# Seven products instead of eight in half of an input stage, with its loads, transposes and side work rearranged

## Chip, cores and metric

The kernel runs on one core of a Trainium2 chip. The metric is the device time of one execution in microseconds (us). Engines are called as the profile calls them: PE (TensorE: matmuls, with its weight loads PEld), DVE (VectorE), ACT (ScalarE), POOL (GpSimd) and SP (SyncE, which here only issues DMAs). Lines L... are lines of the kernel before.

## What is computed

Sparse attention in the shape (4 batches, 8 heads, 768 tokens, head size 64), and behind it a two-layer network with a quick GELU on the 3072 x 512 result. Weights are 512 x 2048 and 2048 x 512. All inputs and the output are float32.

```python
k_sum = k.reshape(B, H, nb, 32, D).max(axis=3)      # one key per block of 32 tokens
v_sum = v.reshape(B, H, nb, 32, D).mean(axis=3)     # one value per block
scores_l = scale * q @ k^T, kept where |pos_q - pos_k| < 16
scores_s = scale * q @ k_sum^T + log(32)
a = softmax(concat(scores_l, scores_s))
x = a @ concat(v, v_sum)                            # heads side by side: 3072 x 512
h = x @ w_in
out = (h * sigmoid(1.702 * h)) @ w_out
```

## The kernel before

Batches are worked through one after the other, and each batch has two stages. The **input stage** multiplies the batch's x (kept transposed, as four tiles `xT`: two halves of 384 tokens, two groups of 256 features) by `w_in`, in 16 column tiles of 128 (`nt`, 0 to 15) for each half, and writes the GELU of it to `gT` as float16. The **output stage** multiplies `gT` by `w_out`, and in its gaps PE does the attention of the next batch (scores, values), so that the next x is there when its input stage begins. Batch 0 is led in by other code, which the change doesn't touch. Every engine runs its instructions in the order in which the code records them (`_Ordered`, L18); only data and buffers make an engine wait.

*Input stage, plain* (`ff_open`, `ff_one`, L666 to L682): for each tile and half four matmuls of 384 columns into one PSUM bank, then a GELU on ACT. Tiles come in pairs (j, j + 8), since the output stage wants sums of such pairs: `g_sums` (L683) makes four sums `gs` of a pair on DVE.

*Input stage, seven products* (`ff_product`, `ff_copy`, L739 to L770; batch 3 alone): a pair of tiles and its two halves is a 2 x 2 block product, and it is done in seven products of two matmuls each, and not in eight, in the manner of Strassen and Winograd. It needs sums of the weights (`wsi`, by `win_sum`, L716), kept where batch 2's keys and queries were (`kx` and `qT` of buffer 0), and sums of the input (`xs`, by `x_sums`, L725), kept where batch 2's values were (`vw` of buffer 0). Of each pair DVE copies one bank to another ("a"), and adds twice (b, c); ACT makes one copy (s) and four GELUs. The PSUM tags are A (3 banks), B (1), C and E (2 each).

*Output stage* (`product`, L775): three token tiles t of 128 rows in each half, seven products of eight matmuls of 256 columns for each, in the order of `seq` (L847). Behind the i-th product, `beside` (L1056) does what `plan` (L1036) lists for slot i: scores ("s"), masks ("m", a DVE multiplication of 128 x 768), values ("v", each followed by normalizations on DVE), transposes of x by DMA ("d").

*What a next batch needs.* GpSimd's queue loads k, q and v with a cast to bfloat16 (`load_batch`, L246: four, four and twelve DMAs). SP's queue turns k and q by DMA transposes (`xk`, `xq`, L567 to L577). `rest_k` (L578) makes the maximum of each key block on DVE and copies halo keys and maxima into place. `value_rows` (L1076) has four halo DMAs, the block sums of the values on PE (`vsum`, L280), their sum on DVE (`block_sums`, L304) and two DMAs that bring them to the value tiles. There are two buffers of keys, queries and values: batch 3 uses buffer 1, batch 2 buffer 0. `gate2` is a one-element copy on GpSimd that makes its queue wait until the copied tile is there, and holds back the loads behind it.

In the kernel before, the main loop (L1123 to L1168) treats batches 1 and 2 alike: a plain input stage, with the block sums of the next batch's values in its second step, and an output stage that loads the batch after next at slot 1 and turns its keys at slots 16 and 18. Batch 2's input stage also begins with the four weight sums for batch 3 on DVE (L1127).

## Time and profile before

| what | value |
|---|---|
| three runs | 205.85, 206.2 and 208.32 us, median 206.2 |
| the profiled execution | 205.39 us, its span 203.4 us |
| granted PE clock | 0.998 |
| PE, DVE, ACT, POOL busy | 97%, 69%, 62%, 44% of the span |
| batch 1's output stage | 96.56 to 119.13 us from the span's start |
| batch 2's input stage | 119.13 to 140.57 us |
| batch 2's output stage | 140.57 to 163.13 us |
| batch 3's input stage, to its first output product | 163.13 to 180.73 us |
| loads | 69648 packets, 13.24 MB on GpSimd's queue |

The span is the time between the first and the last instruction of the profiled execution; the rest of its time lies around it. A row of the chain of waits has start, length (us), engine, output tile and the number of instructions. A row of a group has the operation, output <- input with shapes, count, then busy time and mean ns of one, and the idle time before it with what ended it. A row of the timeline has start, length (us), engine, operation and count, with the idle time before it in brackets. The row of a DMA group has the issuing queue, count, size, and median us from issue to landing.

### The profile page before, as it was taken

To read this page: it belongs to the slowest core of one execution; us is meant where nothing else is said; L and a number is where in the kernel's file an instruction comes from. 1 tells how busy PE (TensorE), PEld (TensorE's weight loads), DVE (VectorE), ACT (ScalarE), POOL (GpSimd) and SP (SyncE) were. 2 spreads that over 40 slices of the span, in tenths; PEclk is the share of its full clock that TensorE was granted. 3 is DMA by queue.
4 is the path that set the end of the run, shared out by engine and by line. 5 is a ranking of instruction groups with operands and counts; after the bars stand their busy time and mean duration, and the time that the engine had idled before them with its cause. 6 is when DMAs were issued, how large, how long until landed. Compare 5 with 4: busy or idle time off the path is not lost.

```text
span 203.4 us, 5851 instructions
## 1 busy us (share of the span) xinstructions
PE 196.7 (97%) x2358; PEld 136.6 (67%) x2358; DVE 141.2 (69%) x391; ACT 125.4 (62%) x240; POOL 89.9 (44%) x141
## 2 busy tenths in 40 slices
PE   6889999999999999999999999999999999999993
PEld 5548655556754566655888876666888865578882
DVE  6586894694856884898767789896769567758221
ACT  4584976638786717777871446778670559984220
POOL 7964489447899584000986034000000009980000
PEclk9999999999999999999999999999999999999999
DMA  5999999999999999999999979999022930000223
GB/s 171 169 165 204 207 207 215 189 156 243 116 122 170 176 170 178 127 165 155 114 181 156 173 140 139 110 247 179 0 104 62 185 119 3 0 0 0 106 105 103
DMA packets 95994, 28.13 MB, mean 138 GB/s; under 512 B 83664, under 2 KB 93152, under 8 KB 95968
## 3 DMA queue, kind: packets, MB, share of 16 engines
q0 software_dynamic: 69648, 13.24, 84.8%
q1 hardware_dynamic: 26176, 14.39, 34.8%
q8 instruction: 18, 0.29, 0.6%
q10 hardware_dynamic: 144, 0.13, 0.2%
q14 instruction: 8, 0.07, 0.1%
HBM read 27.26 MB, written 6.29 MB: 165 GB/s over the span
## 4 chain that ended last, share of the span: by engine, by line
PE 91%; DMA 3%; DVE 3%; issue 1%; ACT 0%; POOLq 0%; DVEq 0%
PE ph L28 32%; PE poA L28 16%; PE po L28 11%; PE poB L28 7%; PE phA L28 4%; PE ps_av L28 4%; PE poC L28 4%; PE ps_s L28 3%; DMA qe<-in_q_dram 3%; DVE ks L28 2%; PE ps_t L28 1%; PE ps_x L28 1%; PE phC L28 1%; PE phB L28 1%; PE phE L28 1%; DVE qT L28 1%
## 5 line engine op out<-in xcount | busy, mean ns | idle before, releaser
L28 PE MATMUL ph<-xT,w_in_sb 128*128 128x384 f16 x400 | 67.8, 326 | 0.1
L28 PEld LDWEIGHTS <-w_in_sb 128*128 128x128 f16 x442 | 42.7, 98 | 27.2 <-issue 0.2
L28 ACT ACTIVATE gT<-ph 128x384 f16<-128x384 f32 x100 | 47.9, 491 | 18.4 <-PE ph L28 17.6
L28 PEld LDWEIGHTS <-gT 128*128 128x128 f16 x312 | 28.8, 98 | 11.3 <-issue 0.2
L28 ACT ACTIVATE a_sb<-ps_s 128x768 bf16<-128x768 f32 (+1 forms) x32 | 25.0, 826 | 12.0 <-PE ps_s L28 12.0
L28 PEld LDWEIGHTS <-gs 128*128 128x128 f16 x288 | 27.7, 98 | 3.4
L28 POOL DMA_DIRECT2D vw<-in_v_dram x36 | 24.6, 699 | 11.9 <-DMA kb<-in_k_dram 5.4
L28 POOL TENSOR_TENSOR gs<-gT 128x384 f16<-128x384 f16 x8 | 7.3, 911 | 43.3 <-ACT gT L28 43.2
L28 PE MATMUL po<-w_out_sb,gT 128*128 128x512 f16 x96 | 23.6, 380 | 0.0
L28 PE MATMUL poA<-ws,gs 128*128 128x256 f16 x144 | 18.7, 273 | 0.0
L28 DVE TENSOR_TENSOR a_sb<-a_sb,mk 128x768 bf16<-128x768 bf16 x28 | 14.9, 554 | 5.5 <-ACT a_sb L28 5.0
L28 DVE TENSOR_TENSOR x<-ps_av,rc 128x384 f16<-128x384 f32 x32 | 17.8, 557 | 1.1
L28 DVE TENSOR_TENSOR gs<-gT 128x384 f16<-128x384 f16 (+1 forms) x34 | 13.3, 390 | 7.2 <-ACT gT L28 6.9
L28 POOL DMA_DIRECT2D qb<-in_q_dram x16 | 15.1, 961 | 2.5 <-DMA w_in_sb<-in_moe_w_in_dram 1.2
L28 PEld LDWEIGHTS <-kx 64*128 64x128 bf16 (+1 forms) x378 | 9.9, 95 | 6.8 <-issue 3.6
L28 POOL DMA_DIRECT2D kb<-in_k_dram x14 | 13.6, 986 | 0.3 <-issue 0.3
L28 DVE TENSOR_REDUCE ks<-kx 128x24 bf16<-128x768 bf16 x12 | 11.4, 948 | 3.4 <-ACT kx L28 3.2
L28 ACT ACT_TABLE_LOAD x10 | 12.8, 1283 | 1.0 <-PEq L1240 0.8
L28 ACT ACTIVATE osb<-poA 128x256 f32<-128x256 f32 x9 | 3.5, 384 | 16.1 <-PE poA L28 16.1
L28 ACT ACTIVATE s<-poA 128x256 f32<-128x256 f32 x11 | 4.2, 385 | 11.2 <-PE poA L28 11.2
L28 PEld LDWEIGHTS <-a_sb 128*64 128x64 bf16 (+2 forms) x400 | 7.9, 108 | 2.8 <-issue 1.3
L28 PE MATMUL poA<-ws,gT 128*128 128x256 f16 x72 | 9.3, 273 | 0.0
(117 smaller groups left out, 288.2 us busy)
## 6 DMA issues: line engine op xcount, KB each, us to landing
out_dram<-osb SPq DMA_DIRECT2D x22, 256.0 KB, 3.9
kb<-in_k_dram POOLq DMA_DIRECT2D x14, 192.0 KB, 6.6
qb<-in_q_dram POOLq DMA_DIRECT2D x12, 192.0 KB, 10.5
vw<-in_v_dram POOLq DMA_DIRECT2D x36, 64.0 KB, 5.5
w_out_sb<-in_moe_w_out_dram POOLq DMA_DIRECT2D x4, 512.0 KB, 12.8
w_in_sb<-in_moe_w_in_dram POOLq DMA_DIRECT2D x3, 512.0 KB, 12.4
vw<-vs SPq DMA_DIRECT2D x6, 198.0 KB, 6.6
gT<-in_k_dram SPq DMA_DIRECT2D x2, 384.0 KB, 3.4
```

Source lines behind the costliest of these rows:

```text
L28: r = f(*a, **kw)
```

## The change

Batch 2's input stage is taken out of the common loop (`in_seven`). Pairs 0 to 3 stay plain, pairs 4 to 7 go by seven products. Seven plain tiles come first; then each pair's products have two plain tiles between them, and one plain tile follows. The PSUM tags A, B, C and E are opened for it, and batch 2's output stage then lives on A (3 banks) and B (1) with two double banks for attention.

Of the four weight sums, the first and the third go to GpSimd in batch 1's output stage (slots 9 and 10); the second and the fourth stay on DVE at the new stage's start, and batch 2's four input sums follow them. The sums `gs` 2 and 3 of six pairs become two long DVE operations in the output stage (`sums23`).

Loads: for batch 2 q comes ahead of v. For batch 3 k waits for the second q transpose of batch 2, q follows k as soon as batch 2's block sums are made, and v is loaded last, at the start of the new stage, after the last x transpose. Batch 2's `value_rows` moves from batch 1's input stage to slot 1 of its output stage; batch 3's halo DMAs and block sums move to slots 1 and 4 of batch 2's output stage. Batch 3's key transposes move from slots 16 and 18 to slots 7 and 8, its halo copies go to GpSimd (`key_halos2`), the copies of the key maxima too, and the masks of its first half (four) as well. `keep_it` gives one copy of the first token tile to ACT.

```diff
@@ load_batch
         if b == 3:
-            pool.tensor_copy(out=gate2, in_=qTs[0][:, 0, 0:1])
+            pool.tensor_copy(out=gate2, in_=qTs[0][:, NP - 1, 0:1])
         load_turned(k, b, kb2, "kb")
         if b == 3:
-            pool.tensor_copy(out=gate2, in_=qTs[0][:, NP - 1, 0:1])
+            pool.tensor_copy(out=gate2[0:32], in_=vs[0:32, H - 1, 0:1])
+        load_turned(q, b, qb2, "qb", (0,) if b == 1 else (0, 1))
+        if b < 3:
+            load_v(b)
         if b == 1:
-            load_turned(q, b, qb2, "qb", (0,))
-        load_v(b)
-        if b < 3:
-            load_turned(q, b, qb2, "qb", (1,) if b == 1 else (0, 1))
+            load_turned(q, b, qb2, "qb", (1,))
@@ keep_it
-            copy(dve if t == 0 and b + 1 < B else act, t_, po)
+            copy(dve if t == 0 and b + 1 < B and name != "s2" else act, t_, po)
@@ the slots of batch 3's attention
+    plan3 = {-1: ["s00", "s01"], 1: ["H"], 2: ["m00", "m01"], 3: ["s02", "s03"], 4: ["R"],
+             5: ["m02", "m03"], 6: ["s10", "s11"], 8: ["m10", "m11", "s12", "s13"], 9: ["m12", "m13"],
...
-                mask(half, i)
+                mask(half, i, pool if b == 3 and half == 0 else dve)
...
+            elif what[0] == "H":
+                halo_dmas(vw[b % 2].rearrange("p (j e) h c -> p j e h c", e=2), 0)
             elif what[0] == "R":
-                value_rows(1)
+                vsum(b % 2, False)
+                block_sums()
+                sum_dmas(vw[b % 2].rearrange("p (j e) h c -> p j e h c", e=2), 0)
@@ batch 2's input stage
+    def in_seven(b, s):
+
+        n = NT // 2
+        xq(0, s)
+        xq(1, s)
+        pool.tensor_copy(out=gate2, in_=xTT[1][1][:, 1, 0:1])
+        load_v(b + 1)
+        key_max2(0, s)
+        win_sum(1)
+        win_sum(3)
+        x_sums(range(4))
+        tiles = [(nt, half) for half in range(2) for nt in (0, n, 1, n + 1)]
+        for p in (2, 3):
+            tiles += [(nt, half) for half in range(2) for nt in (p, n + p)]
+        for tag in "CCEEAAB":
+            plain(*tiles.pop(0), tag)
+        for j in range(4, n):
+            ff_do(j, 1, "a")
+            if j > 4:
+                ff_do(j - 1, "E")
+            ff_do(j, 5, "s")
+            if j > 4:
+                ff_do(j - 1, 4, "A", "g")
+            plain(*tiles.pop(0), "C")
+            if j < 7:
+                key_max2(j - 3, s)
+                key_rows(j - 4, s, ks_of[j - 4], pool)
+            else:
+                key_rows(3, s, ks_of[3], pool)
+                g_sums(2, dve, (0, 1))
+            ff_do(j, 6, "b", 2, "C")
+            plain(*tiles.pop(0), "A")
+            if j < 6:
+                g_sums(j - 4, dve, (0, 1))
+            else:
+                g_sums(j - 6, dve, (2, 3))
+            ff_do(j, 7, "c", 3, "B")
+        ff_do(n - 1, "E")
+        plain(*tiles.pop(0), "A")
+        g_sums(3, dve, (0, 1))
+        ff_do(n - 1, 4, "A")
+        g_sums(n - 1, dve, (0, 1))
@@ the loop over the output stages
-            if i == 0:
-                g_sums(NT // 2 - 1, dve, (2, 3))
-            if nxt:
-                beside(b + 1, i)
-            i += 1
-            if nxt and b + 2 < B:
-                if i == 1:
-                    load_batch(b + 2)
-                if i in (16, 18):
-                    xk(i // 2 - 8, b % 2)
+            if b == 1:
+                if i == 0:
+                    g_sums(NT // 2 - 1, dve, (2, 3))
+                if i == 1:
+                    value_rows(s)
+                    load_batch(b + 2)
+                if i in (7, 8):
+                    xk(i - 7, b % 2)
+                if i in (9, 10):
+                    win_sum(2 * (i - 9), pool)
+                if i in (11, 12):
+                    key_halos2(i - 11, b % 2)
+            elif i in (0, 1):
+                next(bulk)
+            beside(b + 1, i)
```

What the change moves on each engine shows best in the order of its instructions. In these rows `kx_88`, `qT_90` and `vw_92` are buffer 0, `kx_89`, `qT_91` and `vw_93` buffer 1; `xT_98` to `xT_101` are the four tiles of x; `kb` and `qb` hold k and q as loaded, `gate` is the one-element copy.

POOL, from the loads of batch 2 to those of batch 3, before:

```order
L28 DMA kb<-in_k_dram 128x12x64 x4
L28 DMA vw_92<-in_v_dram 64x8x64 x12
L28 DMA qb<-in_q_dram 128x12x64 x4
L28 COPY gate_106<-qT_90 128x1
L28 DMA kb<-in_k_dram 128x12x64 x4
L28 COPY gate_106<-qT_90 128x1
L28 DMA vw_93<-in_v_dram 64x8x64 x12
L28 CAST gate_106<-xT_101 128x1
L28 DMA qb<-in_q_dram 128x12x64 x4
```

and after, from batch 2's q on:

```order
L28 DMA qb<-in_q_dram 128x12x64 x4
L28 DMA vw_92<-in_v_dram 64x8x64 x12
L28 COPY gate_106<-qT_90 128x1
L28 DMA kb<-in_k_dram 128x12x64 x4
L28 COPY gate_106<-vs 32x1
L28 DMA qb<-in_q_dram 128x12x64 x4
L28 TENSOR_TENSOR kx_88<-w_in_sb 128x2048 x2
L28 COPY kx_89<-kx_89 128x2x5x16 x2
L28 COPY kx_89<-kx_89 128x12x2x16
...
L28 CAST gate_106<-xT_101 128x1
L28 DMA vw_93<-in_v_dram 64x8x64 x12
```

Batch 3's q stands ahead of its v, the two weight sums and the halo copies stand between them, and the wait for x comes ahead of v, where it came ahead of q.

SP, from the stores of batch 1's output stage to the transposes of batch 3's keys, before:

```order
L28 DMA out_dram<-osb 128x512 x2
L28 DMA_TRANSPOSE xT_98<-x_2258 128x6x128
L28 DMA out_dram<-osb 128x512
L28 DMA_TRANSPOSE xT_99<-x_2290 128x6x128
L28 DMA out_dram<-osb 128x512
L28 DMA_TRANSPOSE xT_100<-x_2355 128x6x128
L28 DMA_TRANSPOSE xT_101<-x_2387 128x6x128
L28 DMA_TRANSPOSE kx_89<-kb 128x12x64 x4
```

and after:

```order
L28 DMA vw_92<-vs 32x6x528 x2
L28 DMA out_dram<-osb 128x512 x2
L28 DMA_TRANSPOSE kx_89<-kb 128x12x64 x4
L28 DMA_TRANSPOSE xT_98<-x_2259 128x6x128
L28 DMA out_dram<-osb 128x512
L28 DMA_TRANSPOSE xT_99<-x_2291 128x6x128
L28 DMA out_dram<-osb 128x512
L28 DMA_TRANSPOSE xT_100<-x_2362 128x6x128
L28 DMA_TRANSPOSE xT_101<-x_2394 128x6x128
```

The four key transposes stand ahead of all four transposes of x and of two stores, and batch 2's block sums are brought to its values at the head of this piece.

DVE at the start of batch 2's input stage, before:

```order
L28 TENSOR_TENSOR osb<-poB,s_2427 128x256
L28 TENSOR_TENSOR kx_88<-w_in_sb 128x2048
L28 TENSOR_TENSOR kx_88<-kx_88,w_in_sb 128x2048
L28 TENSOR_TENSOR kx_88<-w_in_sb 128x2048
L28 TENSOR_TENSOR qT_90<-w_in_sb,kx_88 128x2048
L28 TENSOR_TENSOR gs<-gT 128x384
L28 TENSOR_TENSOR gs<-gs,gT 128x384
```

and after, up to the last add of the first seven-product pair:

```order
L28 TENSOR_REDUCE ks<-kx_89 128x24
L28 TENSOR_TENSOR kx_88<-kx_88,w_in_sb 128x2048
L28 TENSOR_TENSOR qT_90<-w_in_sb,kx_88 128x2048
L28 TENSOR_TENSOR vw_92<-xT_100,xT_98 128x768
L28 TENSOR_TENSOR vw_92<-xT_101,vw_92 128x768
...
L28 COPY phC<-phA 128x384
L28 TENSOR_REDUCE ks<-kx_89 128x24
L28 TENSOR_TENSOR phB<-phA,vw_92 128x384
L28 TENSOR_TENSOR gs<-gT 128x384
L28 TENSOR_TENSOR gs<-gs,gT 128x384
L28 TENSOR_TENSOR phE<-phA,vw_92 128x384
```

Two weight sums are gone from it, four input sums and a key maximum have come, and the copy and the two adds of a pair stand with a key maximum and two sums between them.

More of the change, by code (lines that the diff above doesn't have):

```diff
@@ new lines, in sums23 @@
+    def sums23(j0):
+        q_ = slice(j0, NT // 2)
+        yield dve.tensor_tensor(out=gs[:, 2, q_], in0=gTb[:, q_, 0:HALF], in1=gTb[:, q_, HALF:S], op=ALU.subtract)
+        yield dve.tensor_tensor(out=gs[:, 3, q_], in0=gTb[:, j0 + NT // 2:NT, 0:HALF], in1=gs[:, 1, q_],
+                                op=ALU.subtract)
+    for b in range(1, B - 1):
+        s = (b + 1) % 2
+        if b == 1:
+            in_plain(b, s)
+        else:
+            mid.close()
+            open_last(ctx, b, (("A", 3), ("B", 1)))
+            with ExitStack() as banks:
+                open_last(banks, b, (("C", 2), ("E", 2)))
+                in_seven(b, s)
+            mid = ExitStack()
+            psb = mid.enter_context(tc.tile_pool(name="psb2", bufs=2, space=bass.MemoryType.PSUM))
+            bulk = sums23(2)
+        exp_soon()
+        beside(b + 1, -1)
+        for i, (t, what) in enumerate(seq):
+            product(b, t, what)
+            if b == 1:
+                if i == 0:
+                    g_sums(NT // 2 - 1, dve, (2, 3))
+                if i == 1:
+                    value_rows(s)
+                    load_batch(b + 2)
+                if i in (7, 8):
[7 more added lines that the diff above has]
+            beside(b + 1, i)
@@ L1170 @@
     mid.close()
[L1171 to L1172 removed]
+    open_last(ctx, B - 1, (("C", 2), ("E", 2)))
     b, n = B - 1, NT // 2
     PLAIN = 1
[L1176 to L1189 removed]
```

109 lines of the change are left out of this document (54 added, 55 removed).

## The prediction

> **What bounds the kernel now.** I read the page's first part, then the chain of waits, then the table by stretches, and last the groups and the timelines around batch 2's input stage.
>
> ```profile
> span 203.4 us, 5851 instructions
> PE 196.7 (97%) x2358; PEld 136.6 (67%) x2358; DVE 141.2 (69%) x391; ACT 125.4 (62%) x240; POOL 89.9 (44%) x141
> PE 91%; DMA 3%; DVE 3%; issue 1%; ACT 0%; POOLq 0%; DVEq 0%
> ```
>
> PE is busy for 97% of the span and is 91% of the chain that ended last. So the work of the other engines is worth nothing by itself; only fewer matmul columns, or a new wait of PE, can move the end. The chain, in order of time, gives the stage that is changed (first the end of batch 1's output stage, then 16 tile pairs, with the block sums of batch 3's values in between), then the first rows of batch 2's output stage and the first values behind it, and last one pair of batch 3, which already uses seven products:
>
> ```profile
> 112.03 0.88 PE ps_av L28 x48
> ...
> 118.26 0.87 PE poA L28 x8
> 119.13 5.20 PE ph L28 x32
> 124.33 0.53 PE ps_vs L28 x48
> 124.86 15.71 PE ph L28 x96
> 140.57 0.46 PE ps_s L28 x24
> ...
> 152.43 0.88 PE ps_av L28 x48
> ...
> 168.70 0.98 PE phA L28 x6
> ...
> 170.98 0.97 PE phA L28 x6
> ```
>
> The pieces follow each other without a gap. The stage's own matmuls take 5.20 + 15.71 = 20.91 us for 128, or 0.163 us each. In batch 3 the same place of the next pair comes 170.98 - 168.70 = 2.28 us later, which is 14 matmuls of 0.163: seven products there run at PE's rate, though each passes through adds on DVE and a copy on ACT.
>
> **The change part by part.** *PE.* Plain, a pair of tiles is 2 tiles x 2 halves x 4 matmuls = 16; by seven products it is 7 x 2 = 14. Four of eight pairs change, so 8 matmuls go: 8 x 0.163 = -1.31 us. The 0.53 us of block sums (twice) move from the input to the output stages, and no other matmul is added: 0. The changed stage is 120 x 0.163 = 19.6 us.
>
> *DVE in the new stage.* The rows that price it:
>
> ```profile
> L28 DVE COPY phC<-phA 128x384 f32<-128x384 f32 x7 | 4.0, 567 | 0.7 <-ACT gT L28 0.6
> L28 DVE TENSOR_REDUCE ks<-kx 128x24 bf16<-128x768 bf16 x12 | 11.4, 948 | 3.4 <-ACT kx L28 3.2
> L28 DVE TENSOR_TENSOR gs<-gT 128x384 f16<-128x384 f16 x33 | 11.7, 355 | 7.2 <-ACT gT L28 6.9
> L28 DVE TENSOR_TENSOR kx<-w_in_sb 128x2048 f16<-128x2048 f16 x2 | 2.4, 1216 | 0.0
> L28 DVE TENSOR_TENSOR vw<-xT,vw 128x768 f16<-128x768 f16 x2 | 1.1, 553 | 0.5 <-DMA xT<-x 0.5
> 118.36 0.42 DVE L28 TENSOR_TENSOR osb<-poB,s 128x256 f32<-128x256 f32 x1 [0.46 <-PE poB L28]
> ```
>
> For each seven-product pair PE has 14 + 8 matmuls (two plain tiles stand among them) = 22 x 0.163 = 3.59 us. DVE has three moves of 0.567, one key maximum of 0.948 and two sums of 0.355: 3.36 us. It fits, with 0.23 us to spare, so the order inside a pair decides. Before the first pair DVE is free at 118.36 + 0.42 = 118.78 and must do a key maximum, two weight sums and four input sums: 0.95 + 2 x 1.22 + 4 x 0.55 = 5.6, until 124.4. PE starts its first product of a pair after seven plain tiles, at 119.13 + 28 x 0.163 = 123.7, ready at 124.0; DVE copies it until 125.0, just as PE, after one product and one plain tile, wants to add to that bank (125.0). Then DVE takes the next key maximum until 125.9 and an add until 126.5, while PE has two products and a plain tile and wants the bank at 126.3: about 0.2 to 0.3 us of PE wait. In the next pair DVE is level again. I take +0.3; the bounds are 0 (as in batch 3) and 4 x 0.3 = 1.2 if each pair slips. ACT's seven activations of a pair fit in the same way (batch 3 has five in 2.28 us, this has seven in 3.59).
>
> *GpSimd.* Two of the four weight sums (128 x 2048 each), the halo copies of batch 3's keys and four masks (128 x 768) come to it, and the two weight sums and four masks leave DVE. The nearest row of such an operation:
>
> ```profile
> L28 POOL TENSOR_TENSOR gs<-gT 128x384 f16<-128x384 f16 x8 | 7.3, 911 | 43.3 <-ACT gT L28 43.2
> 100.39 0.33 POOL L28 COPY gate<-qT 128x1 bf16<-128x1 bf16 x1
> 119.60 0.37 POOL L28 CAST gate<-xT 128x1 bf16<-128x1 f16 x1 [9.75 <-DMA xT<-x]
> ```
>
> By length 2048 / 384 x 0.911 = 4.9 us a weight sum and 1.8 us a mask (estimates). In batch 1's output stage GpSimd now waits for batch 2's block sums (about 100.4), issues four loads of q (four took 4.07) and starts at about 104.6, so both sums stand at 114.4. DVE asks for the first at 119.7: covered by 5 us. The masks run in batch 2's output stage, where the values that need them come 152.43 - 140.57 = 11.9 us behind the stage's start; four take 7.3 us. Covered, cost 0, as long as GpSimd and DVE do not stop each other (a rival, below).
>
> *Queues.* The four key transposes move ahead of the four transposes of batch 2's x on SP's queue. The rows of before, where they came last:
>
> ```profile
> 110.51 1.23 SPq L28 DMA_TRANSPOSE xT<-x  x1
> 112.53 0.33 SPq L28 DMA_DIRECT2D out_dram<-osb  x1
> ...
> 115.28 2.59 SPq L28 DMA_TRANSPOSE xT<-x  x2
> 118.45 6.80 SPq L28 DMA_TRANSPOSE kx<-kb  x4
> ```
> ```profile
> xT<-x SPq DMA_TRANSPOSE x8, 2.8
> vw<-vs SPq DMA_DIRECT2D x6, 198.0 KB, 6.6
> out_dram<-osb SPq DMA_DIRECT2D x22, 256.0 KB, 3.9
> ```
>
> They need 6.80 us of issue. They can start once the store behind product (0, 4) is out, about 105.8, and end at 112.6: the first x transpose is 2.1 us late, the last about 0.5 to 1 us late (118.5), and with 2.8 us of landing the last x is there at about 121.3. PE wants the first half at 119.13 and the second after four more tiles, at 121.7. So it is hidden, with 0.4 us to spare. If the landings double behind the key transposes, up to 2.4 us of PE wait appear: bounds 0 and +2.4, taken +0.1, because q's loads, which run beside them, start earlier than the transposes. The store of the second token tile goes 1.4 us later on the same queue, and DVE waits for its buffer at 117.5: 113.9 + 3.9 = 117.8, a delay of 0.3 on DVE and 0 on PE.
>
> *Values last.* Batch 3's values are now loaded after x has landed, and the block sums follow only in batch 2's output stage. In that stage they end on PE 6.0 us after its start, on DVE about 1.5 later (one copy, four adds), and then two transfers bring the sums to the value tiles, for which PE asks 12.4 us after the start (11.9, and 0.53 for the block sums). That leaves 12.4 - 7.6 = 4.8 us for two issues and the landing. The row above says 6.6 us, beside loads: 6.6 + 0.6 - 4.8 = +2.4 us of PE wait. But nothing else is on the queues by then except stores, which take 2.3 us there:
>
> ```profile
> out_dram<-osb SPq DMA_DIRECT2D x6, 256.0 KB, 2.3
> DMA to landing us min/median/max: 4.7/5.9/10.0
> ```
>
> The first row is of the stretch from 140 to 165 us, the second of all transfers of the sums. Bounds 0 and 2.4; I take +0.2, nearer the quiet row. Batch 2's own sums move to batch 1's output stage in the same way; they start there about 8 us ahead of the values that need them, with q's loads held back behind them: 0.
>
> Sum: -1.31 + 0.3 + 0.1 + 0.2 = -0.7 us. The profiled execution took 205.39 us with its span of 203.4, so it becomes 204.7; against the median of 206.2 it is 205.5, and the profiled execution lies 0.8 under that median. I say 205.4.
>
> **The rivals.** *GpSimd and DVE stop each other (the other side).* The two gate copies of one element above took 0.33 and 0.37 us; a third, with DVE idle of this kind of work, took 0.19. Both slow ones stand beside a DVE operation with two operands from SBUF and end with it:
>
> ```profile
> 95.86 0.19 POOL L28 COPY gate<-qT 128x1 bf16<-128x1 bf16 x1 [17.53 <-DMA qT<-qb]
> 100.13 0.55 DVE L28 TENSOR_TENSOR a_sb<-a_sb,mk 128x768 bf16<-128x768 bf16 x1
> 118.71 1.22 DVE L28 TENSOR_TENSOR kx<-w_in_sb 128x2048 f16<-128x2048 f16 x1
> 106.41 1.26 DVE L28 TENSOR_TENSOR a_sb<-a_sb,mk 128x768 bf16<-128x768 bf16 x2 [1.05 <-ACT a_sb L28]
> ```
>
> 100.13 + 0.55 = 100.68 against 100.72, and 118.71 + 1.22 = 119.93 against 119.97. If it holds the other way round too, DVE's last two masks of batch 2 (106.41) meet the first weight sum (104.6 to 109.5): one runs at 109.5, the other behind the second weight sum at about 114.9. DVE's normalizations queue behind it, and the next values, at 112.03, need the bank that these free: about 115.4 + 0.4 + 1.5 = 117.3, a wait of 5.3 us. If both masks slip in between the two sums it is 112.5, or 0.5 to 1. The masks on GpSimd against DVE's two long sums in batch 2's output stage add 0 to 2. So 205.5 + 5.3 = 210.8, from 206.5 to 212.8. It decides from the point where a GpSimd operation of 4.9 us holds DVE for more than about 2 us. Against it: GpSimd's fifteen sums in batch 3 run at 0.91 beside DVE's work, but that work has one operand in PSUM. No row of before has a long GpSimd operation beside a DVE operation of two SBUF operands.
>
> The Trainium skill, SBUF — State Buffer, section "Who interferes with whom", says that a DVE instruction with two SBUF inputs contends with a GpSimd instruction that reads SBUF, and that the later one blocks until the first has ended. By that rule the upper time of this rival, and not the forecast, is what to expect; the two slow gate copies agree with one direction of it, and no run here shows the other.
>
> *The change gives its gain back on the way.* The three waits above at their upper bounds are 1.2, 2.4 and 2.4 us; any one of them near its bound eats 1.31. Two of them half way give 205.5 + 1.9 = 207.4. For it speaks that DVE has 0.23 us to spare in 3.59; against it that batch 3 shows none of it.
>
> *No wait at all.* -1.31 alone: 204.1 from the profiled execution, 204.9 from the median. Nothing in the chain could give more, so faster by over 2% (4.1 us, about what a measurement of this kernel can tell from no change) needs a gain three times the matmuls that go.
>
> **How the numbers follow.** Forecast, with the case of no wait: 0.58, its own range 204.1 to 206.5. Gain given back: 0.20, 206.2 to 208.6. GpSimd against DVE: 0.20, 206.5 to 212.8, most of it above 210.3. Below 203.9: 0.02. The range of 203.9 to 209.8 leaves out that last case and about three quarters of the third (0.17 in all). Faster by over 2% 0.01, within 2% 0.83 (all but the upper part of the third case), slower by over 2% 0.16.
>
> **What would show it.** In the profile after, the first matmul of batch 2's output stage should come 19.5 to 20.1 us behind the first of its input stage (20.9 + 0.5 before). Waits of PE or of its weight loads for DVE at the first seven-product pair would be my 0.3; at every pair, DVE is the bound. PE waiting at the stage's first tiles for xT means the transposes came late; PE waiting before the first values of batch 2's output stage means the sums landed late. DVE masks of more than 0.6 us, or idle DVE time ended by GpSimd, between 104 and 115 us would show the rival; so would weight sums on GpSimd far from 4.9 us. The forecast is wrong if the four weight and mask operations on GpSimd appear in the chain that ended last.

## The result and the profile after

| | before | after |
|---|---|---|
| median of the runs | 206.02 us (205.56 to 208.32, 4 runs) | 212.77 us (212.67 to 214.15, 4 runs) |
| ratio | | 1.032 (95% interval 1.0232 to 1.0408): slower |
| profiled execution, its span | 205.39, 203.4 | 212.78, 210.7 |
| batch 1's output stage | 22.02 | 29.91 |
| batch 2's input stage | 21.99 | 21.18 |
| batch 2's output stage | 22.01 | 23.21 |

A stage here runs from its first matmul of a product or tile to the first of the next stage, as the timeline of PE shows them (after: 96.12, 126.03, 147.21, 170.42). If nothing waited, the change would give 22.02 + 0.53 = 22.55, 21.99 - 0.53 - 1.31 = 20.15 and 22.01 + 0.53 = 22.54, where 0.53 us are a batch's block sums, and 0.53 would go from batch 1's input stage. So the three stages are 7.4, 1.0 and 0.7 us longer than that. Medians below are over all executions of a run, while ratios leave out those more than 1.5% above its fastest; two experiments have most of their executions in such a longer group, and there both groups are given.

The page of the kernel after: span, busy times, and the granted clock in tenths over 40 slices.

```profile
span 210.7 us, 5848 instructions
...
PE 199.3 (95%) x2350; PEld 137.9 (65%) x2350; DVE 153.4 (73%) x367; ACT 127.1 (60%) x246; POOL 116.3 (55%) x163
...
PEclk9999999999999999999995799999999999999999
```

PE waits over the whole span (producer, us in all, times, longest):

```profile
PE ps_av L28 <- DVE a_sb L28: 4.6, 1, 4.6
...
PE phA L28 <- DVE phE L28: 0.6, 1, 0.6
...
PE ps_av L28 <- DMA vw<-vs: 0.2, 1, 0.2
```

The first is new and the largest: values of batch 2 wait for a masked tile. Timeline of DVE around it, then of GpSimd:

```profile
102.85 0.43 DVE L28 TENSOR_TENSOR osb<-poB,s 128x256 f32<-128x256 f32 x1 [0.52 <-PE poB L28]
103.19 10.15 DVE L28 TENSOR_TENSOR a_sb<-a_sb,mk 128x768 bf16<-128x768 bf16 x1
```
```profile
100.78 4.04 POOL L28 DMA_DIRECT2D qb<-in_q_dram  x4
104.81 8.11 POOL L28 TENSOR_TENSOR kx<-w_in_sb 128x2048 f16<-128x2048 f16 x2
```

One mask, 0.55 us before, takes 10.15 us. It ends at 113.34, 0.42 us behind the second of GpSimd's two sums (104.81 + 8.11 = 112.92). PE stands still, and its clock falls before it goes on (0.80 on average over the wait, 0.50 behind it). The stage in stretches: PE busy with its matmuls, granted clock, packet time as a share of the DMA engines (over 1 where packets overlap), GB/s:

```profile
96.12:108.79 12.67, 12.67 (x238) 1.00 2.25 161
108.79:113.39 4.60, 0.00 (x0) 0.80 1.78 188
113.39:117.93 4.54, 4.54 (x41) 0.50 1.49 109
117.93:126.03 8.10, 8.10 (x114) 0.97 0.94 168
```

The 4.54 us at half the clock are 2.3 more than the same matmuls at full clock. With the wait that is 4.6 + 2.3 = 6.9 of the stage's 7.4.

In the input stage, DVE and GpSimd around PE's wait of 0.62 us:

```profile
136.51 0.82 DVE L28 TENSOR_TENSOR gs<-gT 128x384 f16<-128x384 f16 x1
137.36 0.94 DVE L28 TENSOR_TENSOR gs<-gs,gT 128x384 f16<-128x384 f16 x1
138.23 0.55 DVE L28 TENSOR_TENSOR phE<-phA,vw 128x384 f32<-128x384 f32 x1
```
```profile
136.60 0.44 POOL L28 COPY kx<-ks 128x288 bf16<-128x288 bf16 x1
136.99 1.10 POOL L28 TENSOR_TENSOR gs<-gT 128x384 f16<-128x384 f16 x1
138.17 0.91 POOL L28 TENSOR_TENSOR gs<-gs,gT 128x384 f16<-128x384 f16 x1
```

DVE's sums of 0.355 us grow to 0.82 and 0.94: the first ends (137.33) 0.29 us behind GpSimd's copy (137.04), the second (138.30) 0.21 behind its sum (138.09). The add to phE, for which PE waits, is late by that. Here DVE got its turn between GpSimd's copy and the sum behind it; the mask above had none between two sums.

In the next output stage DVE's first long sum takes 1.35 us and its second 2.46 (1.35 in a run below with these masks on DVE), beside GpSimd's masks:

```profile
150.38 2.46 DVE L28 TENSOR_TENSOR gs<-gT,gs 128x2304 f16<-128x2304 f16 x1
```
```profile
149.76 4.58 POOL L28 TENSOR_TENSOR a_sb<-a_sb,mk 128x768 bf16<-128x768 bf16 x2 [4.27 <-ACT a_sb L28]
```

The first of these two masks takes 1.87 us, until 151.63. DVE's sum ends at 152.84, 1.5 us ahead of the second mask's end: it too had its turn between two GpSimd operations that follow each other. PE waits in this stage only 0.2 us, for the block sums to land. Of the 1.0 and 0.7 us of these two stages, PE's idle time is 0.65 and 0.20 (one gap in the input stage, of 0.04, is not in the list of waits); the rest is matmuls that took longer, and why is open.

### The profile page after: what moved, and what is told of

Same layout as the page of the kernel before. It is cut to its first block, busy times and chain, and to the rows that moved or that the text cites. A ratio compares the mean times of both kernels' runs of the same rounds, so it can differ in the third digit from the quotient of the medians.

```text
span 210.7 us, 5848 instructions
## 1 busy us (share of the span) xinstructions
PE 199.3 (95%) x2350; PEld 137.9 (65%) x2350; DVE 153.4 (73%) x367; ACT 127.1 (60%) x246; POOL 116.3 (55%) x163
## 4 chain that ended last, share of the span: by engine, by line
PE 83%; DVE 9%; DMA 3%; issue 1%; ACT 1%; SPq 0%; DVEq 0%
PE ph L28 26%; PE poA L28 13%; PE po L28 10%; PE phA L28 7%; PE poB L28 7%; DVE a_sb L28 5%; PE ps_av L28 4%; PE poC L28 2%; PE ps_s L28 2%; DMA vw<-vs 2%; PE phC L28 2%; PE phE L28 2%; PE phB L28 2%; DVE ks L28 2%; DMA gT<-in_k_dram 2%
## 5 line engine op out<-in xcount | busy, mean ns | idle before, releaser
L28 PE MATMUL ph<-xT,w_in_sb 128*128 128x384 f16 x336 | 58.5, 326 | 0.1
L28 PEld LDWEIGHTS <-w_in_sb 128*128 128x128 f16 x402 | 38.9, 98 | 25.9 <-issue 1.6
L28 ACT ACTIVATE gT<-ph 128x384 f16<-128x384 f32 x84 | 40.4, 491 | 13.8 <-PE ph L28 13.4
L28 DVE TENSOR_TENSOR a_sb<-a_sb,mk 128x768 bf16<-128x768 bf16 x24 | 23.5, 1004 | 3.9 <-ACT a_sb L28 3.4
L28 POOL TENSOR_TENSOR gs<-gT 128x384 f16<-128x384 f16 x11 | 10.2, 929 | 18.7 <-ACT gT L28 17.3
L28 PE MATMUL poA<-ws,gs 128*128 128x256 f16 x144 | 19.6, 281 | 0.0
L28 PEld LDWEIGHTS <-kx 64*128 64x128 bf16 (+1 forms) x402 | 12.4, 95 | 8.5 <-issue 3.6
L28 ACT ACTIVATE s<-poA 128x256 f32<-128x256 f32 x13 | 5.0, 385 | 20.8 <-DVE osb L28 11.4
L28 DVE TENSOR_TENSOR gs<-gT 128x384 f16<-128x384 f16 (+2 forms) x26 | 12.4, 476 | 6.9 <-ACT gT L28 6.8
L28 PE MATMUL ps_av<-vw,a_sb 128*64 128x65 bf16 x336 | 7.9, 200 | 4.8 <-DVE a_sb L28 4.6
```

The lines of the kernel that those rows point to most:

```text
L28: r = f(*a, **kw)
```

## The experiments

The theory: a DVE operation with two operands in SBUF and a GpSimd operation that reads SBUF exclude each other. Rivals: the issue of q's loads on GpSimd; the load on GpSimd as such; the seven-product stage; the queues.

**The two weight sums back on DVE**

```diff
-                if i in (9, 10):
-                    win_sum(2 * (i - 9), pool)
+                if i in (15, 17):
+                    win_sum(i - 15)
```

> The changed kernel with the two weight sums of batch 1's output stage back on DVE, in slots 15 and 17 of that stage; all else stays, q's loads on GpSimd too. Theory (a GpSimd operation that reads SBUF and a DVE operation with two SBUF operands exclude each other): the masks take 0.55 us each again, PE's wait of 4.6 us and the lowered clock behind it go, 7.0 of the 7.3 us come back: 205 to 206 us. Rival 1 (it is GpSimd's issue of q's loads that holds the mask, which starts at 103.19 while they are issued): the mask stays at several us, the time above 210. Rival 2 (the seven-product stage itself and the late values cost the time): 210 or more, with the masks at 0.55.

Measured: 208.78 us, ratio 1.0119 (1.0032 to 1.0206). Four masks in a row on DVE, beside the same loads of q, then two rows of its stage's end:

```profile
102.69 1.98 DVE L28 TENSOR_TENSOR a_sb<-a_sb,mk 128x768 bf16<-128x768 bf16 x4
```
```profile
116.46 1.21 DVE L28 TENSOR_TENSOR kx<-w_in_sb 128x2048 f16<-128x2048 f16 x1
118.80 0.42 DVE L28 TENSOR_TENSOR osb<-poA,s 128x256 f32<-128x256 f32 x1 [1.12 <-DMA out_dram<-osb]
```

The masks are short again and the 4.6 us are gone: the loads' issue is not the cause, the sums are. But by the ratios (1.032 and 1.0119) only some 4.1 of 6.6 us came back. In their place PE waits 1.71 us for an add of DVE, and that waits for the buffer of a store. SP's queue says why:

```profile
105.51 8.51 SPq L28 DMA_TRANSPOSE kx<-kb  x4
114.15 2.16 SPq L28 DMA_TRANSPOSE xT<-x  x1
116.41 0.52 SPq L28 DMA_DIRECT2D out_dram<-osb  x1
```

The store left at 112.53 before; now it stands behind four key transposes. In the kernel after it was as late, but the stall ahead of it hid that. The seven-product stage adds waits of 0.36 and 0.80 us for phE.

**The two sums on GpSimd, but behind the last mask**

```diff
+                if i == 10:
+                    pool.tensor_copy(out=gate2, in_=a_sb[1, NP - 1][:, 0, 0, 0:1])
+                    win_sum(0, pool)
+                    win_sum(2, pool)
```

> The changed kernel with the same two weight sums on GpSimd, but held behind batch 2's last mask by a one-element copy. Theory: the work of GpSimd is the same (two sums of 4.1 us), only not beside masks; the rest of DVE's work there has one operand in PSUM, so nothing waits: 205 to 206 us, like the kernel with the sums on DVE within 0.5. Rival (GpSimd's load as such, or its sums being ready late, costs the time): 209 or more.

Measured: 210.01 us, 1.019 (1.0114 to 1.0266). The two sums take 8.09 us again, at 108.06, the masks 0.5 each, and no PE wait for a mask is left. The time is the rival's (209 or more), but the wait is another one: PE waits 3.12 us for the store's buffer, since the key transposes took 9.64 us of issue there and the store left at 118.06. The hold of the mask is thus a matter of when GpSimd runs, not of its load; the time is that of the second cause. Whether the sums have a part in the longer issue (8.51 us with the sums on DVE) is open.

**One sum on GpSimd, one on DVE**

```diff
-                if i in (9, 10):
-                    win_sum(2 * (i - 9), pool)
+                if i == 9:
+                    win_sum(0, pool)
+                if i == 15:
+                    win_sum(2)
```

> The changed kernel with only the first of the two weight sums on GpSimd in its old place, the second on DVE in slot 15. Theory: the third mask ends about 0.4 us behind the one sum, near 109.3 instead of 113.3, PE waits 1 to 1.5 us instead of 4.6 and its clock is not lowered: 206 to 207.5 us. Rival (a GpSimd operation of this kind holds DVE whatever its length, or the loss grows with the length alone and the clock has no part): half of 7.3 us, 209 us.

Measured: 209.89 us, 1.0205 (1.0107 to 1.0303). DVE, then GpSimd:

```profile
104.83 6.14 DVE L28 TENSOR_TENSOR a_sb<-a_sb,mk 128x768 bf16<-128x768 bf16 x1
```
```profile
106.45 4.09 POOL L28 TENSOR_TENSOR kx<-w_in_sb 128x2048 f16<-128x2048 f16 x1
```

The mask ends at 110.97, again 0.43 us behind the sum: the hold follows the sums' number. PE waits 0.65 for the mask and then 0.49 and 0.82 us for DVE's normalizations, which I had left out: after a hold DVE has five masks to make up. The stage takes 25.3 us against 29.9; the whole time is 2.4 us above the theory's upper end and nearer the rival's 209; 0.9 of it is the seven-product stage's wait for phE, and 1.1 a wait at 67.7 us for batch 1's block sums to land, which the kernel after, the same up to there, doesn't show.

**PE kept busy through the wait**

```diff
+        if b == 2 and half == 0 and g == 1:
+            for i in range(36):
+                pe.matmul(out=ps[:, 0:256], lhsT=w_out_sb[:, 0, 0:128], rhs=w_out_sb[:, 0, 0:256],
+                          start=True, stop=True, skip_group_check=True)
```

> The changed kernel with 36 extra matmuls of 256 columns (4.7 us at the 0.131 us of such a matmul) on PE ahead of batch 2's second group of values, into the bank that these values then overwrite, so PE works through its wait for the masks. Theory (4.6 us of wait, and some 2.5 us more because the granted clock falls to 0.5 behind it): the masks still take 10 us, the clock stays near 1, 210 to 210.8 us. Rival (the clock is no part, the rest of the loss is DVE's queue of late work): 212.5 to 213.

Measured: 212.33 us, 1.0312 (1.024 to 1.0384): close to the rival. The mask took 10.15 us as before. The stretches from the wait on:

```profile
109.30:114.00 4.70, 4.14 (x43) 3.45 (x36) 4.70 (x2) 0.00 (x0) 4.29 (x2) 1.00 1.73 181
114.00:118.50 4.50, 3.62 (x56) 2.94 (x58) 4.40 (x13) 0.38 (x1) 2.72 (x6) 1.00 0.54 105
```

The clock stays at 1.00, and nothing is won: PE now waits 0.63 us for a mask and 0.73 and 0.82 us for DVE's normalizations, 2.2 in all, where it ran 2.3 us slower in the kernel after. The lowered clock lay in the shadow of DVE's backlog (4.40 of these 4.50 us busy), and its removal alone is worth nothing here.

**The second pair of key transposes later**

```diff
-                if i in (7, 8):
-                    xk(i - 7, b % 2)
+                if i == 7:
+                    xk(0, b % 2)
...
+            if b == 1 and i == 15:
+                xk(1, b % 2)
+                key_halos2(1, b % 2)
```

(with the sums on DVE)

> The kernel with the weight sums on DVE, and the second pair of key transposes behind the last transpose of batch 2's x (slot 15) instead of slot 8, its halo copies with it. In the run with the sums on DVE PE waited 1.71 us for an add of DVE, which waited for the buffer of a store that stood on SP behind four key transposes (issue at 116.41, before at 112.53), and 0.36 us for x. Theory (SP's queue, not the sums, made that wait): the store is issued by about 113, both waits go, 2.0 us less than the run with the sums on DVE: 205.3 to 206 us. Rival (DVE is late by its two sums of 1.2 us, or by the loads that land beside): the wait stays within 0.5 us, 207 us or more.

Measured: 207.65 us, 1.0117 (1.008 to 1.0155). The store left at 113.64, but landed 5.5 us later (2.3 in the run with the sums on DVE), and PE still waited 1.4 us; the wait for x is gone. By its numbers this is the rival: PE's wait for the store changed by 0.3 us, and the ratio not at all. The place on the queue is one half of the wait, the landing the other. That q's loads lengthened the landing is not shown: in two kernels below, the same up to here (one but for GpSimd's writes), the store landed in 2.9 and 4.0 us beside the same loads, and the wait was 0.3.

**What GpSimd operation holds a mask?** Added to the kernel with the transposes split, in slot 9: three operations that only write, or four that read one operand.

```diff
+                if i == 9:
+                    for w in range(3):
+                        pool.memset(kflat[:, w * 2048:(w + 1) * 2048], 0.0)
```
```diff
+                if i == 9:
+                    for w in (0, 1, 2, 0):
+                        pool.tensor_copy(out=kflat[:, w * 2048:(w + 1) * 2048], in_=w_in_sb[:, w])
```

> The kernel with the weight sums on DVE and the key transposes split, and three GpSimd operations added in slot 9 that only write (2048 zeros each, into the memory that the weight sums fill later), some 7 us in all beside the masks. Theory in its narrow form (two operations exclude each other only if both read SBUF, and DVE's with two operands): masks stay at 0.55 us, no PE wait, the time of the kernel without them within 0.5. Rival (any long GpSimd operation holds DVE): a mask of several us and the wait of the changed kernel, 5 us more.

> The same kernel with four GpSimd copies of 2048 elements added in slot 9 instead (one operand from SBUF each, some 8 us in all). Theory (a GpSimd operation that reads SBUF holds a DVE operation with two SBUF operands): one mask lasts until the copies end, as in the changed kernel, and PE waits 3 us or more: 209 us or more. Rival (only GpSimd operations with two operands do it): masks of 0.55 us and the time of the kernel without the copies.

Measured: 206.12 us with the writes, 212.81 with the copies (one run each; 207.65 without either). The time with the writes is 1.5 us below the kernel without them, and not within 0.5: the store's wait is 0.3 there. DVE and GpSimd with the writes:

```profile
105.46 1.26 DVE L28 TENSOR_TENSOR a_sb<-a_sb,mk 128x768 bf16<-128x768 bf16 x2 [1.05 <-ACT a_sb L28]
```
```profile
104.01 5.36 POOL L28 MEMSET kx<- 128x2048 f16 x3
```

and with the copies:

```profile
102.25 9.43 DVE L28 TENSOR_TENSOR a_sb<-a_sb,mk 128x768 bf16<-128x768 bf16 x1
```
```profile
103.84 7.42 POOL L28 COPY kx<-w_in_sb 128x2048 f16<-128x2048 f16 x4
```

Two masks run inside 5.36 us of writes in their usual time (0.56 each). One mask waits through all four copies. So the theory holds in its narrow form, for masks: GpSimd's reads matter, one operand is enough, its writes do not. This is what the Trainium skill says (SBUF — State Buffer, "Who interferes with whom"): a DVE instruction with two SBUF inputs contends with a GpSimd instruction that reads SBUF, not with one that only writes it. The same section says that whichever issues first keeps the port; here the held mask was recorded 1.6 us ahead of the first copy and still waited, so one of the two recorded starts is not the point at which the port is taken.

**GpSimd's work in the seven-product stage left out**

```diff
-                ff_do(j - 1, 4, "A", "g")
+                ff_do(j - 1, 4, "A")
...
-                key_rows(j - 4, s, ks_of[j - 4], pool)
...
-                key_rows(3, s, ks_of[3], pool)
```

> The kernel with the weight sums on DVE and the key transposes split, and with GpSimd's six sums (0.91 us each) and four key rows (0.5 us each) of batch 2's seven-product stage left out, so that these values are stale in the output; the values' loads stay. Theory (DVE's sums of 0.355 us grow to 0.6 to 1.1 beside GpSimd's, and PE's two waits of 0.36 and 0.80 us for DVE's add are their price): all DVE sums of the stage at 0.36, no PE wait there, 1.0 to 1.3 us less than with them: about 204.3 us. Rival (the seven products themselves are too much for DVE): the waits stay, no gain.

Measured: 205.52 us, 1.001 (0.9981 to 1.004), 2.1 us under the kernel with that work. DVE's sums in this stage, mean ns in the second number behind the bar:

```profile
L28 DVE TENSOR_TENSOR gs<-gT 128x384 f16<-128x384 f16 x5 | 1.7, 348 | 0.0
L28 DVE TENSOR_TENSOR gs<-gs,gT 128x384 f16<-128x384 f16 x3 | 1.1, 358 | 0.1
L28 DVE TENSOR_TENSOR gs<-gT,gs 128x384 f16<-128x384 f16 x2 | 0.7, 351 | 0.0
```

In the kernel after the same three rows have 549, 758 and 571 ns. The stage takes 20.11 us, 1.35 less than before without block sums (21.46), and PE waits for DVE nowhere beyond 0.2: the 1.31 us of the eight matmuls are real, and the seven-product pairs are not too much for DVE. Of the 2.1 us, 1.2 are this stage (21.30 with the work), as expected; the rest is the store's wait, 0.3 here and 1.4 there. The whole time of about 204.3 did not come.

**Loads in the order of before, then DVE's sums moved, then the block sums sooner.** Three steps, each on top of the one ahead; all of the work is done.

```diff
-        load_turned(q, b, qb2, "qb", (0,) if b == 1 else (0, 1))
-        if b < 3:
-            load_v(b)
+            pool.tensor_copy(out=gate2, in_=qTs[0][:, NP - 1, 0:1])
+        else:
+            load_turned(q, b, qb2, "qb", (0,) if b == 1 else (0, 1))
+        load_v(b)
```
```diff
             plain(*tiles.pop(0), "C")
-            if j < 7:
-                key_max2(j - 3, s)
...
+            if j < 6:
+                g_sums(j - 4, dve, (0, 1))
...
             ff_do(j, 6, "b", 2, "C")
             plain(*tiles.pop(0), "A")
-            if j < 6:
-                g_sums(j - 4, dve, (0, 1))
+            if j < 7:
+                key_max2(j - 3, s)
```

```diff
-    plan3 = {-1: ["s00", "s01"], 1: ["H"], 2: ["m00", "m01"], 3: ["s02", "s03"], 4: ["R"],
+    plan3 = {-1: ["s00", "s01"], 1: ["H"], 2: ["R", "m00", "m01"], 3: ["s02", "s03"],
...
-                mask(half, i, pool if b == 3 and half == 0 else dve)
+                mask(half, i)
```

> The kernel with the weight sums on DVE and the key transposes split, and batch 3's loads in the order of before: values in batch 1's output stage, q behind batch 2's x, q's transposes behind the second seven-product pair. The block sums stay in batch 2's output stage. Theory (with the split alone the store was issued at 113.64 but took 5.5 us to land beside q's early loads, and GpSimd's key rows and sums ran late, in one bunch, because the twelve value loads stood ahead of them): the wait for the store is at most 0.4 us, GpSimd's work in the seven-product stage starts some 8 us sooner in the stage, its waits fall to 0.3 to 0.9 us, and the 0.2 to 0.4 us of waiting for the block sums goes; 205.5 to 206.5 us. Rival (the DMA engines are as full with the values' loads, so the order of the loads has no part): the store lands in 5 us or more again, PE waits over 1 us, 207 us or more.

> The same kernel with the order of DVE's work in a seven-product pair changed: its sums of two SBUF operands stand ahead of the first add, the key maximum (one operand) behind it, where GpSimd's sums of the pair before run. No work is left out. Theory (only operations that read two SBUF operands collide, so an order that keeps them apart in time is enough): DVE's sums are 0.36 us each again and PE's waits for phE go, 0.5 to 1.0 us less than the kernel without this. Rival (DVE is simply full in this stage): the waits stay within 0.3 us.

> The same again, with batch 3's block sums made in slot 2 of batch 2's output stage instead of slot 4, and its four masks on DVE instead of GpSimd. Theory: the sums land before the values ask for them (0.2 to 0.4 us of wait gone), and DVE's second long sum there takes 1.35 instead of 2.46 us: 0.2 to 0.6 us less. Rival (nothing waits for these, DVE gets 2.2 us of masks in addition): no gain or up to 1 us more.

Measured: 206.5 us, 1.0032 (1.0001 to 1.0063); 206.11, 1.0017 (0.9986 to 1.0048); 206.65, 1.0053 (1.0025 to 1.008). The times of the three are not apart beyond their intervals, so the stages decide. With the loads as before the store's wait is 0.3 us and the longest wait for phE 0.5. But the store, issued at 112.23, took as long to land as with q's loads beside it:

```profile
out_dram<-osb SPq DMA_DIRECT2D x1, 256.0 KB, 5.5
```

So the rival was right about the landing (5 us or more) and wrong about PE's wait: the store left 1.4 us sooner. With DVE's order changed the waits for phE are gone and the stage takes 20.38 us (21.08 without). The reason I gave is only half right: two of the three groups of DVE's sums still take 0.66 and 1.07 us on average; that the sums now stand where DVE has time to spare is argued from the order. The third step lost: PE waits 1.5 us for a bank that the earlier block sums hold.

**The two sums on GpSimd again, behind the value loads and the keys behind x**

```diff
-                if i in (15, 17):
-                    win_sum(i - 15)
+                if i in (9, 10):
+                    win_sum(2 * (i - 9), pool)
```
```diff
-                if i == 7:
-                    xk(0, b % 2)
...
-            if b == 1 and i == 15:
-                xk(1, b % 2)
-                key_halos2(1, b % 2)
+            if b == 1 and i in (16, 18):
+                xk(i // 2 - 8, b % 2)
...
+        key_halos2(0, s)
+        key_halos2(1, s)
...
-            bulk = sums23(2)
+            bulk = sums23(1)
```

> The same again, with the two weight sums of batch 1's output stage on GpSimd once more, in the slots of the changed kernel; but now they stand behind twelve value loads on GpSimd's queue, which issue until about 110, when batch 2's masks are done (107.8). Theory (what costs is the time at which they run, beside masks, not that GpSimd has them): masks of 0.55 us, no PE wait for a mask, the time of the kernel with the sums on DVE within 0.5 us, rather less. Rival (a sum on GpSimd holds DVE's masks as soon as it stands next in the queue, or holds other DVE work): a wait of 2 us or more, 207 us or more.

> The kernel with its loads as before and DVE's sums apart, and now all four key transposes behind the last transpose of batch 2's x, where they were before the change; key maxima one pair later, GpSimd's halo copies behind q's loads, batch 3's masks on DVE, and the two long sums of the next stage over seven pairs instead of six. Theory (the early transposes cost what is still missing, by a store that lands late and by stops of PE): batch 1's output stage as long as before plus its 0.53 us of block sums, the input stage 20.2 to 20.6 against 21.46 before without block sums, 204.3 to 205.2 us, below the kernel before by 0.2 to 0.6%. Rival (the seven-product stage gives no more than it costs on DVE and GpSimd, or the keys now come too late for DVE): level with before or slower, 205.5 us or more.

> The same, with the two weight sums of batch 1's output stage on GpSimd in the changed kernel's slots, behind the twelve value loads on its queue (until about 110, the masks end at 107.8). Theory (what matters is that they run beside no DVE operation with two SBUF operands): masks of 0.55 us, the time of the kernel with the sums on DVE within 0.4 us. Rival (long GpSimd operations hold up something else there, the code or the loads): 1 us or more above it.

Measured: the sums behind the value loads, early keys: 205.3 and 207.3 us in two executions, 209.8 to 216.0 in nine. Keys behind x, sums on DVE: 205.91, 1.0011 (0.9985 to 1.0038), 205.0 to 207.1 in all twelve. The same with the sums on GpSimd: 204.5 to 205.9 in five executions (0.999, 0.9959 to 1.0021), 212.7 to 215.7 in seven. The profiled execution of this last kernel is one of the seven. Its GpSimd, then two masks of DVE:

```profile
103.67 2.06 POOL L28 DMA_DIRECT2D vw<-in_v_dram  x3
105.70 8.12 POOL L28 TENSOR_TENSOR kx<-w_in_sb 128x2048 f16<-128x2048 f16 x2
```
```profile
104.52 9.73 DVE L28 TENSOR_TENSOR a_sb<-a_sb,mk 128x768 bf16<-128x768 bf16 x2
```

The first of the two masks takes 0.55 us, the second the other 9.2. In this execution the twelve value loads were issued by 105.7 instead of about 110, so the sums met the masks. I had counted on the loads as a cover, and they end early in some executions. The early-keys kernel's profile shows another thing: loads until 110.9, masks of 0.56 us, but a stop of 2.73 us of PE in the middle of a product, and why most of its executions were long is open. So both of my expectations for the sums on GpSimd failed for most executions, and the one for the keys behind x, 204.3 to 205.2, by 0.7.

**Sums held, and the rest tuned**

```diff
-        key_halos2(1, s)
...
+            if j == 6:
+                key_halos2(1, s)
...
-    plan3 = {-1: ["s00", "s01"], 1: ["H"], 2: ["m00", "m01"], 3: ["s02", "s03"], 4: ["R"],
+    plan3 = {-1: ["s00", "s01"], 1: ["H"], 3: ["s02", "s03"], 4: ["R", "m00", "m01"],
```

and, in the first of the two, the sums on GpSimd with the one-element copy of the second experiment ahead of them; in the second they are on DVE in slots 15 and 17.

> The kernel with the keys behind x, the two weight sums on GpSimd, and ahead of them a one-element copy from batch 2's last masked tile, so that they start when the masks are done; the halo copies of keys 2 and 3 stand behind the third pair's key rows instead of the first's, and batch 3's first two masks behind its block sums. Theory (the long executions of the kernel without the copy were the mask held by the sums): no execution above 208 us, masks of 0.55 us; and with the sums off DVE and GpSimd's work of the seven-product stage on time, 204.2 to 205.2 us, 0.2 to 0.7% below the kernel before. Rival (long GpSimd operations in this stage hold up something else): executions of 210 us and more are seen again.

> The same, with the two weight sums on DVE in slots 15 and 17 and no such copy. Theory: 0.3 to 0.5 us more than with the sums on GpSimd, since an add of DVE then comes 0.45 us late for PE at the stage's end; no execution above 208 us. Rival (the sums cost the same on either engine once they meet no mask): the two kernels level within 0.2 us.

Measured: held on GpSimd 204.74 us, 0.9974 (0.9949 to 1.0), all twelve executions from 204.1 to 206.2; on DVE 204.60 us, 0.9956 (0.9933 to 0.9978), 203.7 to 205.5. The held sums and the last masks:

```profile
108.62 0.19 POOL L28 COPY gate<-a_sb 128x1 bf16<-128x1 bf16 x1 [2.06 <-DVE a_sb L28]
108.76 8.08 POOL L28 TENSOR_TENSOR kx<-w_in_sb 128x2048 f16<-128x2048 f16 x2
```
```profile
107.22 1.26 DVE L28 TENSOR_TENSOR a_sb<-a_sb,mk 128x768 bf16<-128x768 bf16 x2 [1.05 <-ACT a_sb L28]
```

With the one copy of 0.19 us the long group is gone. The keys behind x with the sums on DVE had none either, and the one long execution with a profile shows the held mask: the sums meeting the masks made the long group, though the other six long executions have no profile, and halo copies and two masks of the next stage moved in the same step. The two kernels are level within 0.2, as the second's rival had it: sums on GpSimd gain nothing over sums on DVE even when they meet no mask. The one with the sums on DVE beats both given kernels, the one before by 0.9 us (0.2 to 0.7%). Its stages take 23.15, 20.21 and 22.66 us, and of PE's waits in them one of 0.3 us is left.

## Why the prediction was wrong

Forecast 205.4 us (203.9 to 209.8), measured 212.77. By its steps:

- *Eight matmuls fewer, -1.31.* Right: 20.11 against 21.46 us where nothing disturbs, -1.35.
- *GpSimd's sums: "Covered, cost 0, as long as GpSimd and DVE do not stop each other".* This is the step that failed. Its condition was false, as the rival had it. Cost in batch 1's output stage: 4.60 us of wait, and 2.2 to 2.3 more, which are DVE's backlog of masks and normalizations (at full clock PE waits for it, at half clock PE is no faster than it). A sum took 4.09 us instead of the estimated 4.9.
- *The rival GpSimd against DVE, 210.8 (206.5 to 212.8).* Right in kind and place, and its 5.3 us of wait is near the 4.60. It held a different mask: not the last two, one behind each sum, but the third, which is recorded 1.6 us ahead of the first sum and was held through both. The kernel before has four masks there that I left out, and a sum from 104.6 already falls among them:

```profile
103.31 2.05 DVE L28 TENSOR_TENSOR a_sb<-a_sb,mk 128x768 bf16<-128x768 bf16 x4
```

  That its upper end of 212.8 is the measured time is luck: it holds 2 us for GpSimd's masks against DVE's long sums, which cost PE nothing, and not DVE's backlog of 2.2 to 2.3. I gave it 0.20 because "No row of before has a long GpSimd operation beside a DVE operation of two SBUF operands". But two gate copies ended with such an operation, 0.04 us behind it, and nothing spoke against it except rows with one operand in PSUM. The rule of the Trainium skill (SBUF — State Buffer, "Who interferes with whom"), which the prediction cites, allows those rows and says what the rival says. The rival should have been the likeliest.
- *"a delay of 0.3 on DVE and 0 on PE" for the store behind the key transposes.* Mis-sized, and hidden in the result. The four transposes took 8.5 to 9.6 us of SP instead of 6.80, while q's loads ran, and PE waited 1.7 and 3.1 us as soon as the masks were right. The landing, taken as 3.9 us, was 2.3 to 5.5.
- *Key transposes ahead of x, +0.1.* Right for x: PE's tiles waited 0.36 us once, else 0.
- *DVE at the first seven-product pair, +0.3.* The wait was not there: the first pair passes without one. It came later, 0.62 us at the second pair in the kernel after and 1.16 at the third and fourth with the sums on DVE. GpSimd's sums beside DVE's made it (it is gone without them), and the forecast's sum has no term for that.
- *Block sums landing late, +0.2.* Right: 0.2 us.
- *Masks on GpSimd in the next stage, 0.* Right for PE, though DVE's long sum grew from 1.35 to 2.46 us.

What stays open: why the hold begins ahead of GpSimd's recorded start, why the mask had no turn between GpSimd's operations while DVE's sums in the later stages had, and what makes the loads' issue end at 105.7 in one execution and at 110.9 in another.

## What to carry to other kernels

Before work goes from DVE to GpSimd, list what DVE does in that time: a DVE operation with two operands in SBUF can wait for GpSimd operations that read SBUF, for one of them or, as the masks here, for up to four that follow each other (7.42 us), and all that queues behind it on DVE waits as well. Time GpSimd's work by a dependence (a copy of one element from the tile that must be done first), not by other work ahead of it on the queue, whose end varies. And when the largest wait is removed, read the profile again: of 6.6 us lost, some 4.1 came back with the sums, and a store behind early transposes and sums colliding in the next stage stood behind it.

## What the runs showed of the chip that was not expected

- A wait of PE of 3.1 us (the sums behind the last mask) left the granted clock at 1.00; 3.9 us (the copies) and 4.6 us (the kernel after) were followed by 0.50 for at least 4.5 us. But a stop of 2.73 us, in the kernel with the sums behind the value loads and early keys, was followed by 0.50 as well (columns as in the stretches of the result):

```profile
114.43:117.16 2.73, 0.00 (x0) 0.98 2.07 116
117.16:120.50 3.34, 3.34 (x16) 0.50 1.22 295
```

  So here the length of the stop alone did not decide. The Trainium skill (TensorE: Matmul & The Clock Gate, "HAM oscillation — how this bites in real kernels") sets the limit at gaps of about 3.4 us; the waits of 3.1, 3.9 and 4.6 us agree with it, the stop of 2.73 us does not.
- PE stopped in the middle of a product, with no semaphore in sight, in some kernels while loads were running. Timeline of PE in the kernel with its loads as before:

```profile
113.43 0.60 PE L28 MATMUL poB<-ws,gs 128*128 128x256 f16 x4
114.80 0.60 PE L28 MATMUL poB<-ws,gs 128*128 128x256 f16 x4 [0.78 <-issue]
```

The trace has a 16 KB packet on the queue of kind instruction from 111.6 to 113.1, 1.7 us ahead of the restart; with GpSimd's writes it ended at 111.9 and PE went on at 113.7. That these stops are PE's code coming late is argued from the two, not shown.
- A store of 256 KB at the same place of two programs that are the same up to there landed in 4.0 us in one and in 5.5 in the other; in a second such pair (loads as before, with and without DVE's sums moved) in 5.5 and 3.4.
